# An attention, dense and expert kernel: two exponentials, value loads and mixing matrices issued in another order, and the routing's sums and counting rearranged

## The chip, the cores and the metric

The kernel runs on one core of a Trainium2 chip. The metric is the device time of one execution in microseconds. Kernels are compared by the median of several runs. All times below are of one core; the profile is of one execution, taken by the hardware profiler.

## The reference: what is computed

Three stages follow each other, all in FP32.

```
scores = q @ k.T / 8                      # 4 batches, 12 heads, 448 rows, 64 wide
scores = einsum("bhij,hg->bgij", scores, w_pre)
attn   = softmax(scores)
attn   = einsum("bhij,hg->bgij", attn, w_post)
x      = attn @ v                         # rows become 1792 tokens of 768
h      = x @ w_in                         # 768 -> 2048
x      = where(h > 0, h, exp(h) - 1) @ w_out          # 2048 -> 768
compute = x @ w_skip > 0
e       = argmax(x @ w_gate)              # 8 experts
out     = x;  for tokens with compute:
out    += prob[e] * (relu(x @ w1[e]) @ w2[e])         # 768 -> 1024 -> 768
```

The heads are mixed by two 12 x 12 matrices, once before and once after the softmax. A token with a skip score of zero or less passes unchanged; all others go to the one expert with the largest logit.

## The kernel before, in words

**Precision.** A matrix is held as two parts, a high one and the rest, and a product is three matmuls (high with high, high with low, low with high: `THREE`, L38). Splitting is a cast on ScalarE and a subtraction on VectorE or GpSimd.

**Attention** (L72 to L430) goes through tiles of 120, 120, 120 and 88 query rows of each batch, and each tile in three periods (48 periods). The scores of a tile (`qk`, L144, six matmuls for each of two heads, two PSUM tiles) are written to `s` and brought by DMA into a layout where rows and heads share the partitions (`d`, `relayout`, L183). A period handles up to two pairs of blocks, `cur[0]` and `cur[1]`. For each pair: `mix_pre` (L201) multiplies by the first mixing matrix (`kpre_low`, `kpre_up`) into PSUM tiles `c`; `top` (L211) takes row maxima on VectorE (`nmx`); `softmax` (L218) takes two exponentials on ScalarE (`e`, with the sums `sm`); `norm` (L227) scales the second mixing matrix by the sums (`kr`). In the next period `mix_post` (L240) multiplies `e` by `kr` into `f`, and two copies, one on ScalarE and one on VectorE, put it into `at` (L258). Between the second pair and its `norm` the same loop issues the `qk` of a later tile, and then `av` (L261), the product with the values `v`. The PSUM tiles of `c` and `qk` share one pool of five buffers, `ps_w` (L101): a period takes eight, so the last `qk` tiles use buffers that this period's exponentials have just read.

All loads, relayouts and stores are issued by SyncE (SP) in the order of the program. At the start SyncE issues the loads of q and k, of the mixing matrices and of all v of the first batch (L333); `kron` (L299) and L355 to L366 build the mixing matrices on VectorE and GpSimd after the first tile's scores.

**The dense stage.** h is computed in groups of 128 features by 448 tokens (`products`, L579; 18 matmuls each). The weights come as 64 bit floats, `narrowing` (L480) makes FP32 of them (`a`, `p`, `wf`), `split` (L460) the two parts. `split_x` (L521) splits the tokens `x` into `xh`.  The order of the first eight groups is written out by hand (L666 to L697).

**The second dense product and the routing** (L703 to L908) go through 14 tiles of 128 tokens. A tile has 16 chunks of six matmuls (`o`, L859), and its results are copied to `x2` by ScalarE. Weights that did not stay on the chip come back through DRAM (`wr`, L804). During a tile the one before it is routed: `score` (L740 on) makes nine sums of 768 products each, six on VectorE (L755), three as a product on GpSimd (L748) and a sum on ScalarE (L749); `route` (L759 on) finds the best expert, a one-hot row `oh` (L776), and counts how many tokens went to each expert so far with two matmuls `pp` (L778, L779); the slots are then written to DRAM by an indirect DMA (L797). The tiles 12 and 13 alternate by chunks at the end. For the last two tiles the first expert's tokens are not fetched back: one-hot matrices `hot` and transposes (`tx`, `pt`) place them, and the older ones come by a gather `xp` (L864) from rows that the slots name (`pre`, L877).

From the second dense product on a scheduler sets the order of the instructions on each engine from their dependences and its own estimates; up to group 7 of the dense stage the program's order stands.

**The experts** follow, with weights `w1t` loaded ahead.

Of the kernel before, what the change touches and what calls it, by code (L numbers as in the profile page):

```python
# [20 lines left out]
NK = DM // 128  # L21
# [27 lines left out]
AT_SCORE, AT_ROUTE, AT_FIRST = 8, 18, 11  # L49

# [21 lines left out]
def attention(tc, q, k, v, w_pre, w_post, xT, mix):  # L72
# [12 lines left out]
    with ExitStack() as ctx, ExitStack() as mixing, ExitStack() as scoring:  # L85
# [175 lines left out]
        def av(T, u, ps=None):  # L261
# [15 lines left out]
            for p in (2 * u, 2 * u + 1):  # L277
                if b + 1 < B and it == len(ROWS) - 1:
                    load_v(b + 1, p)
# [7 lines left out]
        stores = []  # L287
# [45 lines left out]
        for p in range(NK):  # L333
            load_v(0, p)
        moves = []
        for p in range(NK):
            if p + 1 < NK:
                if p % 2:
                    split_q(0, p // 2 + 1)
                split_k(0, p + 1, nc.vector)  # L340
            move = qk(0, p)
            if p > 0:
                moves.pop()()
            moves.append(move)
        moves.pop()()
# [6 lines left out]
        kpre = kron(pre, "kpre", False)  # L352
        kpost = kron(post, "kpost", True)

        kpre_low = const.tile([UP, UP], FP32, name="kpre_low")  # L355
        nc.vector.memset(kpre_low, 0.0)
        nc.sync.dma_start(out=kpre_low[GAP:, GAP:], in_=kpre[:HP, :HP])
        kpre_up = const.tile([128, UP], FP32, name="kpre_up")
        nc.sync.dma_start(out=kpre_up[UP:UP + HP, :], in_=kpre[:HP, :UP])
        kposts = [const.tile([128, HP], FP32, name=f"kpost{z}") for z in range(2)]  # L360
        for t in kposts:
            nc.vector.memset(t, 0.0)
        nc.vector.tensor_copy(out=kposts[1][:HP].rearrange("p (g i) -> p g i", g=H),
                              in_=kpost[:HP].rearrange("p (g i) -> p g i", g=H)[:, :, :HR])
        for z, first in ((1, UP), (0, GAP), (0, UP + GAP)):
            nc.sync.dma_start(out=kposts[z][first:first + HP, :], in_=kposts[1][:HP, :])  # L366
# [5 lines left out]
        for n in range(NP):  # L372
# [11 lines left out]
            if late:  # L384
                next(mix)
            if T2 < len(tiles):
                if u2 == 0:
                    load_q(T2)
                if tiles[T2][1] == 0:
                    load_k(tiles[T2][0], 2 * u2)  # L390
                    load_k(tiles[T2][0], 2 * u2 + 1)
            scores = []
            for i in range(2):
                mix_pre(cur[i])
                if i == 0 and n + 2 < NP:
                    relayout(units[n + 2][0])
                moves = mix_post(old[i]) if old else []
                top(cur[i])
                if old:
                    moves[1](nc.scalar.copy)  # L400
                    moves[0](nc.vector.tensor_copy)
                softmax(cur[i])
                if i == 1 and T < len(tiles):
                    scores = [qk(T, 2 * u), qk(T, 2 * u + 1)]
                if late:
                    next(mix)
# [28 lines left out]
def mixtures(tc, order, xT, w_in, w_out, w_skip, w_gate, w1, w2, ident, gT, wf, wg, x2d, slots, out):  # L435
# [5 lines left out]
    with ExitStack() as top:  # L441
# [27 lines left out]
        with ExitStack() as ctx:  # L469
            f64_p = pool("f64", 2, ctx, side="right")  # L470
            cv_p = pool("cv", 1, ctx, side="right")
            xr_p = pool("xr", 6, ctx, side="right")
# [193 lines left out]
            narrowed[1] = narrow(raws.pop(1))  # L666
            raws["out"] = load_w_out(0)
            products(1)
            split_x(2, range(3), both)
            elu(1)  # L670
            wi[1] = split(narrowed.pop(1), ring_a)
            split_x(2, range(3, 6), both)
# [33 lines left out]
        with ExitStack() as ctx:  # L706
# [33 lines left out]
            def score(x2, cols=slice(0, DM)):  # L740
# [3 lines left out]
                for e in range(E + 1):  # L744
                    w = wrow[:, e, cols]
                    if e % 3 == 0:
                        p = st_p.tile([128, DM], FP32, tag="prod", name="prod", bufs=2)
                        nc.gpsimd.tensor_tensor(out=p[:, :n], in0=x2, in1=w, op=ALU.mult)  # L748
                        nc.scalar.activation(out=p[:, :n], in_=p[:, :n], func=ACTF.Copy, accum_out=lg[:, e:e + 1])  # L749
                    else:  # L750
                        if part == 0:
                            t = st_p.tile([128, DM], FP32, tag="junk", name="junk", bufs=1)
                        o = part * n
                        part = (part + 1) % (DM // n)
                        nc.vector.scalar_tensor_tensor(out=t[:, o:o + n], in0=x2, scalar=1.0, in1=w, op0=ALU.mult,  # L755
                                                       op1=ALU.mult, accum_out=lg[:, e:e + 1])
                return lg

            def route(i, lg):  # L759
# [16 lines left out]
                nc.vector.tensor_scalar(out=oh, in0=iota8, scalar1=ef, scalar2=do, op0=ALU.is_equal, op1=ALU.mult)  # L776
                pp = ps_r.tile([128, 512], FP32, tag="r", name="pp")
                nc.tensor.matmul(out=pp[:, :E], lhsT=ones, rhs=seen, start=True, stop=False)  # L778
                nc.tensor.matmul(out=pp[:, :E], lhsT=upper, rhs=oh, start=False, stop=True)  # L779
# [68 lines left out]
            for i, n, fc, cs in work:  # L848
# [24 lines left out]
                if i and n == (15 if i == 1 else AT_ROUTE if last else 11):  # L873
                    hot = old_hot = route(i - 1, scored if last else score(rows[i - 1]))
# [7 lines left out]
                if fc == NF - 1:  # L882
                    if 0 in cs:
                        x2 = rows[i] = x2_p.tile([128, DM], FP32, tag="x2", name="x2")
                    for c in cs:
                        to, at = x2[:, cols[c]], po[c][:, :cols[c].stop - cols[c].start]
                        if last and c == 0:
                            nc.vector.tensor_copy(out=to, in_=at)
                        else:
                            nc.scalar.copy(out=to, in_=at)  # L890
# [9 lines left out]
            hot = route(NTILE - 1, lg)  # L900
# [416 lines left out]
```

## Time and profile before

| | |
|---|---|
| median of 3 runs | 1108.67 us (1106.9 to 1115.65) |
| the profiled execution | 1108.77 us, span 1107.0 us |
| mean granted clock of TensorE | 0.981 |
| TensorE busy | 1024.1 us, 93% |
| VectorE busy | 802.3 us, 72% |
| ScalarE busy | 566.7 us, 51% |
| GpSimd busy | 390.7 us, 35% |
| attention | to about 400 us |
| first dense product | about 400 to 652 us |
| second dense product, routing | about 652 to 924 us |
| experts | about 924 to 1107 us |

A matmul row counts an engine as busy while a matmul runs; matmuls on different halves of the array can run side by side. The idle time in front of an instruction is put down to the instruction of another engine, or the DMA, that came last among those it waited for. Times in rows are microseconds from the start of the span.

### The profile page before, as it was taken

What the parts mean: (1) busy time and instruction counts of PE and PEld (TensorE: products, weight loads), DVE (VectorE), ACT (ScalarE), POOL (GpSimd) and SP (SyncE); (2) the same over time, 40 slices, a digit from 0 to 9 for tenths busy, and PEclk for the clock granted to TensorE, in tenths of its full rate; (3) what the DMA queues carried; (4) which work ended last, traced back from release to release, by engine and by line L of the source; (5) the groups of instructions that cost most, each with busy time, mean ns of one, the idle gap of its engine ahead of it and who ended that gap; (6) DMA issues with size and microseconds to landing.
All of it is one profiled execution on the core that took longest, in us unless ns stands there. A gap on an engine that the chain in (4) does not pass through costs nothing. (4 is left out here: it accounts for less than half of the span.)

```text
span 1107.0 us, 29935 instructions
## 1 busy us (share of the span) xinstructions
PE 1024.1 (93%) x12082; PEld 882.8 (80%) x12082; DVE 802.3 (72%) x1495; ACT 566.7 (51%) x1150; POOL 390.7 (35%) x355
## 2 busy tenths in 40 slices
PE   6998999899899888999999999999999989899997
PEld 4676667666677667899999988999999978788887
DVE  5775777677577668667666557878787856999953
ACT  5664656466465555444544454333333326677751
POOL 2232214123221226232232202535354534756521
PEclk8999999999999999999999999999999998999999
DMA  6453564465455556555566557733333385999800
GB/s 202 170 173 109 164 202 138 131 195 182 110 165 173 166 153 225 171 170 157 193 215 206 178 171 262 237 94 107 96 105 107 94 317 184 392 391 343 328 8 32
DMA packets 134218, 199.67 MB, mean 180 GB/s; under 512 B 35860, under 2 KB 101400, under 8 KB 133821
## 3 DMA queue, kind: packets, MB, share of 16 engines
q1 hardware_dynamic: 131933, 191.27, 52.4%
q0 software_dynamic: 2144, 6.46, 1.6%
q8 instruction: 96, 1.57, 0.6%
q14 instruction: 45, 0.37, 0.1%
HBM read 122.47 MB, written 37.65 MB: 145 GB/s over the span
## 5 line engine op out<-in xcount | busy, mean ns | idle before, releaser
L859 PE MATMUL o<-w,gh 128*128 128x384 f32 (+2 forms) x1344 | 242.5, 339 | 2.9 <-ACT w L463 2.4
L585 PE MATMUL h<-xh,w 128*128 128x448 f32 x1152 | 236.3, 367 | 4.7 <-POOL xh L519 4.7
L859 PEld LDWEIGHTS o<-w,gh 128*128 128x128 f32 x1344 | 234.1, 190 | 7.3 <-ACT w L463 3.6
L585 PEld LDWEIGHTS h<-xh,w 128*128 128x128 f32 x1152 | 216.9, 189 | 23.4 <-POOL xh L519 6.5
L236 POOL TENSOR_SCALAR kr<-kpost,rs 128x60 f32<-128x60 f32 x180 | 77.4, 444 | 284.5 <-DVE rs L232 242.7
L252 PEld LDWEIGHTS f<-kr,e 64*64 64x64 f32 (+2 forms) x5760 | 121.2, 138 | 54.6 <-issue 33.5
L755 DVE SCALAR_TENSOR_TENSOR junk<-x,wrow 128x768 f32<-128x768 f32 x78 | 117.1, 1501 | 40.0 <-ACT x L890 38.6
L252 PE MATMUL f<-kr,e 64*64 64x60 f32 (+2 forms) x5760 | 122.4, 225 | 7.3 <-DVE at L258 1.8
L500 POOL TENSOR_TENSOR wf<-a,p 128x768 f32<-128x768 f32 x32 | 66.6, 2082 | 163.3 <-DVE p L498 122.8
L215 DVE TENSOR_REDUCE nmx<-c 128x1 f32<-128x448 f32 x180 | 104.5, 620 | 25.9 <-PE c L206 25.9
L258 ACT COPY at<-f 128x480 f32<-128x480 f32 x96 | 52.5, 547 | 135.2 <-PE f L252 135.2
L1029 DVE TENSOR_TENSOR wlo<-w1t,whi 128x1536 fp32r<-128x1536 f32 x50 | 111.6, 2255 | 13.6 <-ACT whi L1026 13.6
L224 ACT ACTIVATE e<-c,nmx 128x448 f32<-128x448 f32 x180 | 113.0, 637 | 6.3 <-DVE nmx L215 6.3
L1026 ACT CAST whi<-w1t 128x1536 fp32r<-128x1536 f32 x64 | 94.3, 1483 | 34.1 <-PE ph L1056 17.5
L748 POOL TENSOR_TENSOR prod<-x,wrow 128x768 f32<-128x768 f32 x39 | 93.9, 2434 | 50.0 <-ACT x L890 26.8
L154 PE MATMUL qk<-k,qq 64*120 64x448 f32 (+1 forms) x576 | 90.6, 404 | 17.3 <-ACT e L224 10.3
L206 PE MATMUL c<-d,kpre_up 60*64 60x448 f32 x336 | 85.1, 574 | 11.7 <-ACT s L158 11.7
L274 PE MATMUL xp<-at,v 128*64 128x120 f32 (+3 forms) x1536 | 92.2, 267 | 1.4 <-DVE at L258 1.4
L274 PEld LDWEIGHTS xp<-at,v 128*64 128x64 f32 (+1 forms) x1536 | 75.1, 137 | 21.9 <-issue 17.3
L159 DVE TENSOR_SCALAR s<-qk 120x448 f32<-120x448 f32 (+1 forms) x96 | 58.3, 618 | 45.0 <-PE qk L154 19.8
L206 PE MATMUL c<-d,kpre_low 64*64 64x448 f32 x336 | 84.3, 554 | 3.5 <-DMA kpre_low<-kpre_kr 3.5
L154 PEld LDWEIGHTS qk<-k,qq 64*120 64x120 f32 (+1 forms) x576 | 52.8, 180 | 42.1 <-ACT e L224 25.2
(185 smaller groups left out, 1449.2 us busy)
## 6 DMA issues: line engine op xcount, KB each, us to landing
w1t<-in_moe_w_dram SPq DMA_DIRECT2D x64, 768.0 KB
d<-s SPq DMA_DIRECT2D x168, 210.0 KB
gT<-g SPq DMA_DIRECT2D x64, 224.0 KB
f<-in_moe_w_in_dram SPq DMA_DIRECT2D x16, 768.0 KB
f<-in_moe_w_out_dram SPq DMA_DIRECT2D x16, 768.0 KB
gr<-gT SPq DMA_DIRECT2D x48, 256.0 KB
rk<-in_k_dram SPq DMA_DIRECT2D x24, 224.0 KB
xr<-xT SPq DMA_DIRECT2D x24, 224.0 KB
```

The lines of the kernel that those rows point to most:

```text
L154: nc.tensor.matmul(out=ps[:n, :S], lhsT=qt[T, p // 2][rows, a, p % 2, :n], rhs=kt[b, p][rows, z, :], start=(i == 0), stop=(i == 2))
L206: nc.tensor.matmul(out=ps[j * UP:(j + 1) * UP, :S], lhsT=kpre_up[UP:UP + HP, :] if z else kpre_low if len(U) == 2 else kpre[:d[z, j].shape ...
L215: nc.vector.tensor_reduce(out=t, in_=c, op=ALU.max, axis=AX.X, negate=True)
L224: nc.scalar.activation(out=e, in_=c, func=ACTF.Exp, bias=t, accum_out=sms[U][:, i:i + 1])
L252: nc.tensor.matmul(out=ps[to, c // 2, :, z, :], lhsT=e[rows, keys], rhs=kr[rows, :])
L274: nc.tensor.matmul(out=ps[z * 64:(z + 1) * 64, i, :n], lhsT=t[:, z, jc % t.shape[2], :], rhs=att[T][:t.shape[0], jc, 2 * p + z, :n], start ...
L585: nc.tensor.matmul(out=ps, lhsT=w[:, a, kk, :], rhs=xs[tb, kk][:, z, :], start=(kk == 0 and a + z == 0), stop=(kk == NK - 1 and a == 1))
L748: nc.gpsimd.tensor_tensor(out=p[:, :n], in0=x2, in1=w, op=ALU.mult)
L755: nc.vector.scalar_tensor_tensor(out=t[:, o:o + n], in0=x2, scalar=1.0, in1=w, op0=ALU.mult, op1=ALU.mult, accum_out=lg[:, e:e + 1])
L859: mm = nc.tensor.matmul(out=po[c][:, :cols[c].stop - cols[c].start], lhsT=gs[i][fc // GC][:, a, fc % GC, :], rhs=wo[fc][:, z, cols[c]], st ...
L1026: nc.scalar.copy(out=hi, in_=t)
L1029: (nc.vector if dve else nc.gpsimd).tensor_tensor(out=lo, in0=t, in1=hi, op=ALU.subtract)
```

## The change

In attention, three things move. The loads of v are put on a list (`values`) and issued in the next period, behind that period's relayouts and stores and ahead of the loads of q and k; for the first batch this is behind the relayouts of the first two periods. The mixing matrices are built within the loop of the first tile's scores. And for the second pair of a period the two exponentials are issued ahead of the copy `at<-f` on ScalarE.

In the dense stage the pool `xr` has nine buffers instead of six, and all of `split_x(2)` stands ahead of the second weight block's `narrow`. In the routing all nine sums are made on VectorE; `route` is cut in two, and its second part `seat`, with the counting matmuls, comes at chunk 15 instead of 11 (for the last tile both stay at 18); the last tile's first copy of `x` goes from VectorE to ScalarE.

```diff
@@ attention
+                values.append((b + 1, p))          # was: load_v(b + 1, p)
...
-        for p in range(NK):
-            load_v(0, p)
+        values += [(0, p) for p in range(NK)]
         for p in range(NK):
...
             moves.append(move)
+            if p == 2:
+                kpre = kron(pre, "kpre", False)
+                kpost = kron(post, "kpost", True)
...
         split_q(1, 1)
-        kpre = kron(pre, "kpre", False)
-        kpost = kron(post, "kpost", True)
...
         relayout(units[1][0])
@@ the loop over periods
                 next(mix)
+            while values:
+                load_v(*values.pop(0))
             if T2 < len(tiles):
...
                 moves = mix_post(old[i]) if old else []
                 top(cur[i])
+                if i == 1:
+                    softmax(cur[i])
                 if old:
                     moves[1](nc.scalar.copy)
                     moves[0](nc.vector.tensor_copy)
-                softmax(cur[i])
+                if i == 0:
+                    softmax(cur[i])
@@ the dense stage
-            xr_p = pool("xr", 6, ctx, side="right")
+            xr_p = pool("xr", 9, ctx, side="right")
...
-            narrowed[1] = narrow(raws.pop(1))
             raws["out"] = load_w_out(0)
             products(1)
-            split_x(2, range(3), both)
+            split_x(2, range(6), both)
+            narrowed[1] = narrow(raws.pop(1))
             elu(1)
             wi[1] = split(narrowed.pop(1), ring_a)
-            split_x(2, range(3, 6), both)
             load_x(3)
@@ score: all nine sums
-                    if e % 3 == 0:
-                        p = st_p.tile([128, DM], FP32, tag="prod", name="prod", bufs=2)
-                        nc.gpsimd.tensor_tensor(out=p[:, :n], in0=x2, in1=w, op=ALU.mult)
-                        nc.scalar.activation(out=p[:, :n], in_=p[:, :n], func=ACTF.Copy, accum_out=lg[:, e:e + 1])
-                    else:
...
+                    nc.vector.scalar_tensor_tensor(out=t[:, o:o + n], in0=x2, scalar=1.0, in1=w, op0=ALU.mult,
+                                                   op1=ALU.mult, accum_out=lg[:, e:e + 1])
@@ route is cut in two
+                return i, oh, do
+
+            def seat(i, oh, do, after=None):
                 pp = ps_r.tile([128, 512], FP32, tag="r", name="pp")
...
-                if i and n == (15 if i == 1 else AT_ROUTE if last else 11):
-                    hot = old_hot = route(i - 1, scored if last else score(rows[i - 1]))
+                if i and n == (AT_ROUTE if last else 11):
+                    routing = route(i - 1, scored if last else score(rows[i - 1]))
+                if i and n == (AT_ROUTE if last else AT_SEAT):
+                    hot = old_hot = seat(*routing, None if last else mm)
...
-                        if last and c == 0:
-                            nc.vector.tensor_copy(out=to, in_=at)
-                        else:
-                            nc.scalar.copy(out=to, in_=at)
+                        nc.scalar.copy(out=to, in_=at)
```

The order of ScalarE in one period of attention, before (`at<-f` is the copy of the finished product, `e` an exponential, `s` a copy of scores, `qq` a split of q):

```order
L258 COPY at<-f 128x48x10
L224 ACTIVATE e,sm<-c,nmx 128x448 x2
L258 COPY at<-f 128x48x4
L224 ACTIVATE e,sm<-c,nmx 128x448 x2
L158 ACTIVATE s<-qk 120x448 x2
L141 CAST qq<-rq 128x240
```

and now:

```order
L259 COPY at<-f 128x48x10
L225 ACTIVATE e,sm<-c,nmx 128x448 x4
L259 COPY at<-f 128x48x10
L159 ACTIVATE s<-qk 120x448 x2
L142 CAST qq<-rq 128x240
```

All four exponentials now stand together, and the second copy `at<-f` behind them.

The order of SyncE at the start, before, from the last load of v on (`d` are relayouts of scores, four for a first pair; `kpre` and `kpost` parts of the mixing matrices):

```order
L125 DMA v<-in_v_dram 64x128
L193 DMA d_154<-s 120x1x448
L193 DMA d_155<-s 120x1x448
L193 DMA d_156<-s 120x1x448
L193 DMA d_157<-s 120x1x448
L112 DMA rq<-in_q_dram 128x720
L357 DMA kpre_low<-kpre_kr 60x60
L359 DMA kpre_up<-kpre_kr 60x64
L366 DMA kpost_330<-kpost_330 60x60
L366 DMA kpost_329<-kpost_330 60x60 x2
L193 DMA d_158<-s 120x1x448
```

and now, from the last part of the mixing matrices on:

```order
L360 DMA kpost_252<-kpost_253 60x60 x2
L194 DMA d_154<-s 120x1x448
L194 DMA d_155<-s 120x1x448
L194 DMA d_156<-s 120x1x448
L194 DMA d_157<-s 120x1x448
L113 DMA rq<-in_q_dram 128x720
L194 DMA d_158<-s 120x1x448
L194 DMA d_159<-s 120x1x448
L194 DMA d_160<-s 120x1x448
L194 DMA d_161<-s 120x1x448
L126 DMA v<-in_v_dram 128x384
```

The five DMAs of the matrices now stand ahead of the first `d`, and the twelve loads of v behind the eighth.

The order of VectorE in a token tile of the routing, before, from the slots on (`gh` is a split of the next tile's input, `junk` a sum):

```order
L796 CAST si<-slot 128x1
L736 TENSOR_TENSOR gh<-gr,gh 128x512
L755 SCALAR_TENSOR_TENSOR junk,lg<-x_11734,wrow 128x768
L736 TENSOR_TENSOR gh<-gr,gh 128x512
L755 SCALAR_TENSOR_TENSOR junk,lg<-x_11734,wrow 128x768 x3
L736 TENSOR_TENSOR gh<-gr,gh 128x512
L755 SCALAR_TENSOR_TENSOR junk,lg<-x_11734,wrow 128x768 x2
L761 MAX mx<-lg 128x8
```

and now:

```order
L802 CAST si<-slot 128x1
L755 SCALAR_TENSOR_TENSOR junk,lg<-x_11713,wrow 128x768
L741 TENSOR_TENSOR gh<-gr,gh 128x512
L755 SCALAR_TENSOR_TENSOR junk,lg<-x_11713,wrow 128x768 x3
L741 TENSOR_TENSOR gh<-gr,gh 128x512
L755 SCALAR_TENSOR_TENSOR junk,lg<-x_11713,wrow 128x768 x4
L741 TENSOR_TENSOR gh<-gr,gh 128x512
L755 SCALAR_TENSOR_TENSOR junk,lg<-x_11713,wrow 128x768
L761 MAX mx<-lg 128x8
```

Nine sums stand where six stood; the fourth `gh` of a tile is ahead of this piece in both.

## Rows read from the trace of the kernel before

**Rows 1.** The page, part 1: busy us (share of the span) and instructions of TensorE.

```profile
PE 1024.1 (93%) x12082; PEld 882.8 (80%) x12082; DVE 802.3 (72%) x1495; ACT 566.7 (51%) x1150; POOL 390.7 (35%) x355
```

**Rows 2.** The waits of TensorE: released by what, us in total, times, longest.

```profile
engine line waited for: us in total, times, longest us
...
PE qk L154 <- ACT e L224: 10.3, 31, 0.4
PE pp L779 <- DVE oh L776: 8.3, 10, 1.5
...
PE h L585 <- POOL xh L519: 4.7, 3, 4.1
PE tx L844 <- DVE load L930: 4.6, 1, 4.6
PE c L206 <- DMA kpre_low<-kpre_kr: 3.5, 1, 3.5
...
PE o L859 <- ACT w L463: 2.4, 3, 1.9
```

**Rows 3.** Time line of TensorE, a period with the wait: start, us, instructions, [idle before].

```profile
126.44 1.07 PE L154 MATMUL qk<-k,qq 64*120 64x448 f32 x7
127.84 0.88 PE L154 MATMUL qk<-k,qq 64*120 64x448 f32 x5 [0.32 <-ACT e L224]
128.64 0.59 PE L274 MATMUL xp<-at,v 128*64 128x88 f32 x9
```

**Rows 4.** The same, a period without the wait.

```profile
92.93 1.48 PE L154 MATMUL qk<-k,qq 64*120 64x448 f32 x12
94.34 0.84 PE L274 MATMUL xp<-at,v 128*64 128x120 f32 x12
```

**Rows 5.** Time line of ScalarE and VectorE in the period of rows 3.

```profile
125.27 1.16 DVE L215 TENSOR_REDUCE nmx<-c 128x1 f32<-128x448 f32 x2
...
125.58 0.64 ACT L224 ACTIVATE e<-c,nmx 128x448 f32<-128x448 f32 x1
...
126.60 0.57 ACT L258 COPY at<-f 128x480 f32<-128x480 f32 x1 [0.29 <-PE f L252]
...
127.06 0.63 ACT L224 ACTIVATE e<-c,nmx 128x448 f32<-128x448 f32 x1
...
127.68 0.64 ACT L224 ACTIVATE e<-c,nmx 128x448 f32<-128x448 f32 x1
```

**Rows 6.** Time line of SyncE at the start: DMA issues.

```profile
7.45 6.93 SPq L125 DMA_DIRECT2D v<-in_v_dram  x12
...
18.77 0.85 SPq L357 DMA_DIRECT2D kpre_low<-kpre_kr  x1
```

**Rows 7.** Time line of ScalarE, first token tile of the second dense product.

```profile
661.25 1.68 ACT L463 CAST w<-wr 128x768 fp32r<-128x768 f32 x2 [1.62 <-DMA wr<-wf]
```

**Rows 8.** Stretches: busy us and instructions of each engine, granted clock, DMA share, GB/s.

```profile
core 0: us, PE busy (x) PEld busy (x) DVE busy (x) ACT busy (x) POOL busy (x), PEclk, DMA share, GB/s
...
705.70:709.10 3.40, 3.40 (x12) 3.40 (x11) 2.56 (x6) 1.32 (x2) 0.00 (x0) 0.50 0.87 253
...
742.40:760.50 18.10, 17.35 (x100) 17.26 (x100) 14.57 (x31) 6.12 (x15) 8.59 (x4) 1.00 0.34 101
```

**Rows 9.** Groups by line, VectorE, one token tile (742.5 to 760.6): busy us, mean ns.

```profile
L755 DVE SCALAR_TENSOR_TENSOR junk<-x,wrow 128x768 f32<-128x768 f32 x6 | 8.9, 1483 | 3.2 <-ACT x L890 3.1
```

**Rows 10.** Line 755 over the whole kernel: ns of one, minimum/median/maximum.

```profile
L755 DVE SCALAR_TENSOR_TENSOR junk<-x,wrow x78: 946/959/2620, 678.4 to 909.6; 128x768 f32<-128x768 f32 x78
```

**Rows 11.** Time lines of GpSimd and VectorE in one token tile.

```profile
711.70 7.37 POOL L748 TENSOR_TENSOR prod<-x,wrow 128x768 f32<-128x768 f32 x3 [1.09 <-ACT x L890]
...
717.42 2.47 DVE L755 SCALAR_TENSOR_TENSOR junk<-x,wrow 128x768 f32<-128x768 f32 x1
```

**Rows 12.** Time lines of GpSimd, VectorE and TensorE at the end of the routing.

```profile
899.39 1.05 POOL L864 DMA_INDIRECT xp<-x2d,pre  x1 [6.69 <-DMA pre<-slots]
...
910.49 0.68 DVE L888 COPY x<-o 128x512 f32<-128x512 f32 x1
...
916.26 0.41 PE L830 MATMUL pt<-ident,xp 128*128 128x128 f32 x1
```

**Rows 13.** DMA issues from 888 to 925: median us from issue to landing.

```profile
xp<-x2d,pre POOLq DMA_INDIRECT x1, 7.4
```

More of the change, by code (lines that the diff above doesn't have):

```diff
@@ L49 @@
 AT_SCORE, AT_ROUTE, AT_FIRST = 8, 18, 11
+AT_SEAT = 15
 R0, RC, LOOK = 3, 2, 2
@@ L285, in av @@
             return move
-        stores = []
+        stores, values = [], []
         def store():
@@ L344, in attention @@
             moves.append(move)
+            if p == 2:
+                kpre = kron(pre, "kpre", False)
+                kpost = kron(post, "kpost", True)
+                kpre_low = const.tile([UP, UP], FP32, name="kpre_low")
+                nc.vector.memset(kpre_low, 0.0)
+                nc.sync.dma_start(out=kpre_low[GAP:, GAP:], in_=kpre[:HP, :HP])
+                kpre_up = const.tile([128, UP], FP32, name="kpre_up")
+                nc.sync.dma_start(out=kpre_up[UP:UP + HP, :], in_=kpre[:HP, :UP])
+                kposts = [const.tile([128, HP], FP32, name=f"kpost{z}") for z in range(2)]
+                for t in kposts:
+                    nc.vector.memset(t, 0.0)
+                nc.vector.tensor_copy(out=kposts[1][:HP].rearrange("p (g i) -> p g i", g=H),
+                                      in_=kpost[:HP].rearrange("p (g i) -> p g i", g=H)[:, :, :HR])
+                for z, first in ((1, UP), (0, GAP), (0, UP + GAP)):
+                    nc.sync.dma_start(out=kposts[z][first:first + HP, :], in_=kposts[1][:HP, :])
         moves.pop()()
@@ L351, in attention @@
         split_q(1, 1)
-        kpre = kron(pre, "kpre", False)
-        kpost = kron(post, "kpost", True)
[L355 to L366, printed above, removed]
         relayout(units[1][0])
@@ L745, in score @@
                     w = wrow[:, e, cols]
-                    if e % 3 == 0:
-                        p = st_p.tile([128, DM], FP32, tag="prod", name="prod", bufs=2)
-                        nc.gpsimd.tensor_tensor(out=p[:, :n], in0=x2, in1=w, op=ALU.mult)
-                        nc.scalar.activation(out=p[:, :n], in_=p[:, :n], func=ACTF.Copy, accum_out=lg[:, e:e + 1])
-                    else:
[L751 to L756, printed above, removed]
+                    if part == 0:
+                        t = st_p.tile([128, DM], FP32, tag="junk", name="junk", bufs=1)
+                    o = part * n
+                    part = (part + 1) % (DM // n)
+                    nc.vector.scalar_tensor_tensor(out=t[:, o:o + n], in0=x2, scalar=1.0, in1=w, op0=ALU.mult,
+                                                   op1=ALU.mult, accum_out=lg[:, e:e + 1])
                 return lg
@@ L776, in route @@
                 nc.vector.tensor_scalar(out=oh, in0=iota8, scalar1=ef, scalar2=do, op0=ALU.is_equal, op1=ALU.mult)
+                return i, oh, do
+            def seat(i, oh, do, after=None):
                 pp = ps_r.tile([128, 512], FP32, tag="r", name="pp")
-                nc.tensor.matmul(out=pp[:, :E], lhsT=ones, rhs=seen, start=True, stop=False)
-                nc.tensor.matmul(out=pp[:, :E], lhsT=upper, rhs=oh, start=False, stop=True)
+                with behind(after):
+                    nc.tensor.matmul(out=pp[:, :E], lhsT=ones, rhs=seen, start=True, stop=False)
+                with behind(after):
+                    nc.tensor.matmul(out=pp[:, :E], lhsT=upper, rhs=oh, start=False, stop=True)
                 nc.vector.tensor_tensor(out=seen, in0=seen, in1=oh, op=ALU.add)
@@ L899, in mixtures @@
                             nc.sync.dma_start(out=out[i * 128:(i + 1) * 128, :], in_=x2)
-            hot = route(NTILE - 1, lg)
+            hot = seat(*route(NTILE - 1, lg))
             place_old(range(5, NK))
```

1 line of the change is left out of this document (removed).

## The prediction

> **What bounds the kernel now.** I read the page first, then the waits of TensorE, then the time lines around the longest of them. The page says that TensorE is busy for 1024.1 us of 1107.0 [rows 1], so at most 83 us can come from its idle time, unless matmuls that count as busy become shorter. The waits [rows 2] put names to the idle time that this change can reach: qk for an exponential (10.3 us, 31 times), the counting matmul pp for the one-hot row oh (8.3, 10 times), h for xh (4.7), tx in the tail (4.6), c for kpre_low (3.5), o for the split weights w (2.4). All other engines matter only where one of these waits ends on them.
>
> **The exponential in attention.** This term is the largest, and the 10.3 us of the waits is not its size. In a period that does not stall, the twelve qk matmuls start at 92.93 and the next work at 94.34, 1.41 us later [rows 4]; they run in pairs side by side. In a period that stalls, seven start, the eighth waits 0.32, and the next work starts at 128.64, 2.20 us after 126.44 [rows 3]: the wait also breaks the pairs apart. So one stall costs 2.20 - 1.41 = 0.79 us, and 31 of them 24.5 us.
>
> What ends it: the eighth matmul needs the PSUM buffer that the first exponential of the second pair reads (127.06, 0.63 long, ending 127.69; the matmul starts 0.15 later) [rows 3, 5]. Ahead of that exponential ScalarE waits for f and makes a copy at<-f (126.60, 0.57) [rows 5]. The change puts both exponentials ahead of this copy. The first can then start when the exponential before it lets it, 0.62 us after 125.58 (the pitch of 127.06 to 127.68), at 126.20; the maxima are no hindrance, since the first of the two that take 1.16 us from 125.27 is done about 125.9 [rows 5]. It ends at 126.83, and the buffer is free at 126.98. Without a stall the eighth matmul pairs with the seventh, which is due 0.71 us into the group, at 127.15 (the pitch of 1.41 us in six pairs, the first of them longer; an estimate from rows 4). The margin is 0.17 us, small, but the periods repeat alike.
>
> What is late next is the copy: after two exponentials it runs from 127.43 to 128.00. Values' matmuls would now start at 126.44 + 1.41 = 127.85. In every third period they read the tile that this copy completes, and wait some 0.24 us with the release; 10 such periods give back 2.4 us. The two copies of qk behind it start by 127.9 instead of 128.37, so they are not later. The term is -24.5 + 2.4 = **-22.1**. Its bounds are -24.5 (no new wait) and about -8 (the release comes late and only the 0.3 us of idle of each stall is won, less the 2.4).
>
> **The start.** Before, SyncE issues twelve loads of v in 6.93 us ahead of the d relayouts, and kpre_low at 18.77, for which TensorE waits 3.5 us [rows 2, 6]. The change puts the mixing matrices first (five DMAs, some 0.8 us each by the distance in rows 6) and v behind the d of the first two periods. The wait for kpre_low goes, but VectorE and the d relayouts get the matrices' operations ahead of them, and the 6.93 us of v now stand ahead of the d of the third period. Bounds: -3.5, the whole wait, and +3.5, a new wait of that size there. I take **-0.5**.
>
> **The dense stage's first sums.** TensorE waits 4.7 us for xh [rows 2], which GpSimd makes behind wf. The change makes all six xh first. Then wf, and with it the split of the second weight block, comes later, and the fourth product needs that one. So most of the wait moves to the weights: **-1**, between -4.7 and +1.
>
> **The reloaded weights.** ScalarE's cast w waits 1.62 us for the DMA wr<-wf [rows 7], which SyncE issues behind the last gT stores. With the first tile's work in another order these loads go out between those stores, ahead of the last one. I count the whole 2.4: **-2.4**, at worst 0.
>
> **The sums and the counting.** A token tile takes 18.10 us, of which TensorE works 17.35 and VectorE 14.57 [rows 8]; the 0.75 that TensorE lacks are the wait for oh. The change gives VectorE nine sums instead of six, takes three products from GpSimd, and puts pp four chunks (24 matmuls of 17.35/96 = 0.18 us, 4.3 us) later. What a sum costs: 0.959 us in the median and 2.62 at most [rows 10]; six make 8.9 us in a tile [rows 9], and the long ones lie beside the GpSimd products: 2.47 us at 717.42, while three products run for 7.37 us from 711.70 [rows 11]. These products go, so I price all nine at 0.96: 14.57 - 8.9 + 9 x 0.96 + 3 x 0.08 = 14.6 us, without counting that gh gets faster too. Sums start about 0.9 us into the tile, so oh is ready by 15.5, ahead of pp near 17.3. The wait goes: **-8.3** (10 waits). The first long one of these is followed by 3.40 us at half clock (0.50, 1.2 GHz) [rows 8], which would take half that at full: **-1.7**, at worst 0.
>
> **The tail.** TensorE waits 4.6 us for tx; the engine named is VectorE's `load`, but what tx reads is the copy x<-o, which VectorE reaches at 910.49 behind six sums [rows 2, 12]. On ScalarE it comes some 3.9 us sooner (4.6 less a copy of 0.68). But the counting of tile 11 also falls 8 chunks back here, since two tiles alternate: 48 x 0.18 = 8.7 us. The gather xp, issued at 899.39 and 7.4 us on its way, then lands at 899.39 + 8.7 + 7.4 = 915.5, and pt<-xp, before at 916.26, could run at 912.4 [rows 12, 13]. So about 3 of the 3.9 us become a wait for the gather: **-1**, between -5 and +5 (a later gather, and a slow clock after the wait).
>
> **Sum:** -22.1 - 0.5 - 1 - 2.4 - 8.3 - 1.7 - 1 = -37.0. The profiled execution took 1108.77 us (span 1107.0), 0.1 above the median of 1108.67, so no correction: 1108.8 - 37.0 = **1071.8**, I say 1072. The experts behind it are gated by the routing and should only start earlier.
>
> **The rivals.**
> *The stall in attention moves and stays (chance 0.13).* ScalarE's copy at<-f, or its copies of qk behind it, hold values' matmuls or the next c by as much as the exponential held qk. For it: ScalarE does the same work in the same period, and the margin was 0.17 us. Against: two periods in three do not read that copy at once, and the copies of qk come no later than before. The -22.1 becomes about 0 to -3: 1092.
>
> *VectorE becomes the bound in routing (0.04; the other side).* Its place is each of the 12 tiles from 690 to 905. The budget is 14.57 - 8.9 + 9t + 0.24 with t the price of a sum; it passes TensorE's 17.35 at t = 1.27 us. At today's mean of 1.48 [rows 9] it is 19.2, which is 1.9 x 12 = 23 us dearer than the forecast, 1095: no change by much. From t = 1.6 the change is slower. Were half of the nine as long as 2.47 us [rows 11], t is 1.71, a tile takes 21.3, and the time is 1072 + 3.95 x 12 = 1119. Against it: half of today's sums take no more than 0.959 us [rows 10], and the products, beside which the long one stands [rows 11], are what goes. The Trainium skill (Perfetto Trace Analysis, Identifying the Most-Contended Engine) takes an engine's occupancy as a fair measure of how near VectorE is to its limit and would have the fullest engine relieved first. By that rule a VectorE at 14.57 of 18.10 should get no third more sums, and it would choose this rival. Another page (SBUF — State Buffer, Who interferes with whom) has a VectorE instruction with two SBUF inputs contend with a GpSimd instruction that reads SBUF, which speaks for the short price; here no row shows nine sums without products.
>
> *The edges give back (0.11).* The v loads hold the third period (+3.5 instead of -0.5) and the gather comes late with a slow clock (+5 instead of -1): 1072 + 4 + 6 = 1082.
>
> **How the numbers follow.** The forecast has 0.72. Its own bounds reach from 1062 (no wait at the copy, the tail and the start at their good ends) to about 1083. The range goes up to 1092 to take in the third rival and the middle of the first; what is left out is the rest of the first, the second, and sums beyond the bounds below. A measurement of this kernel tells about 1% from no change, 11 us: all but the second rival, and the worst of the first, are faster by more. Faster 0.93, same 0.04, slower 0.03.
>
> **What would show it.** Right: qk no longer among the waits, twelve qk in 1.41 us, attention shorter by about 22 us; sums of 0.96 without exception; no wait for oh before the last tiles and a tile of 17.35 us; tx without its 4.6 us, and pt<-xp waiting for the gather instead. Wrong: values' matmuls or c waiting for ScalarE's copies 0.5 us or more in each period; sums above 1.3 us; a wait for d near 32 us above 3; o waiting for gh because VectorE is full.

## The result and the profile after

The changed kernel takes 1084.36 us in the median of 4 runs (1082.25 to 1085.37); before takes 1111.3 in 4 runs. The ratio is 0.9745, 95% interval 0.9705 to 0.9785: faster, and inside the range of 1062 to 1092, but 12 us above the forecast of 1072 and just outside the forecast's own bounds (1062 to about 1083): the range holds it because it was widened for the rivals. The profiled execution has a span of 1082.3 us, 24.7 less than before, where 37.0 were forecast.

The page, part 1, and the waits of TensorE in the changed kernel (columns as in [rows 1, 2]):

```profile
PE 1017.3 (94%) x12082; PEld 884.1 (82%) x12082; DVE 778.0 (72%) x1573; ACT 531.6 (49%) x1073; POOL 301.1 (28%) x315
```

```profile
engine line waited for: us in total, times, longest us
PE c L207 <- ACT s L159: 14.0, 4, 4.0
PE pt L836 <- DMA xp<-x2d,pre: 6.2, 1, 6.2
...
PE h L591 <- ACT w L469: 3.3, 1, 3.3
...
PE c L207 <- DMA d<-s: 2.3, 1, 2.3
PE xp L275 <- ACT at L259: 1.8, 4, 1.0
...
PE f L253 <- issue: 1.7, 4, 0.6
...
PE o L865 <- ACT w L469: 0.9, 1, 0.9
...
PE qk L155 <- ACT e L225: 0.5, 2, 0.4
```

The waits for `oh` (8.3 us) of [rows 2] are gone, and so are those for `kpre_low` and `tx`; of those for `e` (10.3) 0.5 us is left, in the first period. New at the top stand the gather `xp` (6.2), a fourth wait of `c` for ScalarE's copy of scores, and `d`; h waits for weights instead of xh.

The period of [rows 3, 5], now; first TensorE, then ScalarE:

```profile
128.64 1.49 PE L155 MATMUL qk<-k,qq 64*120 64x448 f32 x12
130.06 0.45 PE L275 MATMUL xp<-at,v 128*64 128x88 f32 x6
```

```profile
128.38 0.65 ACT L225 ACTIVATE e<-c,nmx 128x448 f32<-128x448 f32 x1
...
129.00 0.65 ACT L225 ACTIVATE e<-c,nmx 128x448 f32<-128x448 f32 x1
...
129.60 0.59 ACT L259 COPY at<-f 128x480 f32<-128x480 f32 x1
130.05 1.02 ACT L159 ACTIVATE s<-qk 120x448 f32<-120x448 f32 x2
```

Twelve qk in one piece, 1.42 us to the next work instead of 2.20. The first exponential of the second pair starts 0.26 us ahead of the qk group, where it stood 0.62 us behind its start.

A token tile of the routing, and the sums over the whole kernel (columns as in [rows 8, 10]):

```profile
709.20:726.38 17.18, 17.18 (x103) 17.18 (x102) 12.74 (x38) 3.64 (x9) 1.43 (x1) 1.00 0.36 108
```

```profile
L755 DVE SCALAR_TENSOR_TENSOR junk<-x,wrow x117: 947/957/1008, 660.0 to 880.8; 128x768 f32<-128x768 f32 x117
```

A tile takes 17.18 us instead of 18.10, without idle time on TensorE. No sum is longer than 1.01 us, and VectorE is busy for less (12.74 us) with nine sums than it was with six (14.57).

To see where the 12 us went I took the same matmul in both traces (their counts agree for every kind) and noted by how much the changed kernel is ahead of it:

| from / to (time before) | ahead at its end | this piece | forecast for it |
|---|---|---|---|
| start to qk of the fourth period (45.4) | +3.7 | +3.7 | -2.1 (-0.5, and two stalls of 0.79) |
| to the first h (399.8) | -10.5 | -14.2 | -20.5 (the rest of -22.1) |
| to the fifth group of h (429.3) | -10.3 | +0.2 | -1 |
| to the last h (650.0) | -11.4 | -1.1 | 0 |
| first tile, reloaded weights (674.8) | -13.9 | -2.6 | -2.4 |
| tiles 1 to 11 (873.6) | -27.0 | -13.0 | -10.0 (-8.3 and -1.7) |
| tail, to the first expert matmul (924.4) | -24.8 | +2.1 | -1 |
| experts | -24.8 | 0.0 | 0 |

Three pieces lost against the forecast, the start 5.8, attention 6.3 and the tail 3.1 us; the tiles won 3.0 more.

### The profile page after: what moved, and what is told of

It is laid out like the page before. It is cut to its first block, busy times and chain, and to the rows that moved or that the text cites. A ratio compares the mean times of both kernels' runs of the same rounds, so it can differ in the third digit from the quotient of the medians.

```text
span 1082.3 us, 29868 instructions
## 1 busy us (share of the span) xinstructions
PE 1017.3 (94%) x12082; PEld 884.1 (82%) x12082; DVE 778.0 (72%) x1573; ACT 531.6 (49%) x1073; POOL 301.1 (28%) x315
## 5 line engine op out<-in xcount | busy, mean ns | idle before, releaser
L865 PE MATMUL o<-w,gh 128*128 128x384 f32 (+2 forms) x1344 | 238.9, 337 | 1.3 <-ACT w L469 0.9
L253 PEld LDWEIGHTS f<-kr,e 64*64 64x64 f32 (+2 forms) x5760 | 124.3, 139 | 56.3 <-issue 38.5
L237 POOL TENSOR_SCALAR kr<-kpost,rs 128x60 f32<-128x60 f32 x180 | 80.1, 459 | 274.9 <-DVE rs L233 212.1
L253 PE MATMUL f<-kr,e 64*64 64x60 f32 (+2 forms) x5760 | 126.1, 226 | 6.7 <-issue 1.7
L755 DVE SCALAR_TENSOR_TENSOR junk<-x,wrow 128x768 f32<-128x768 f32 x117 | 111.8, 956 | 5.6 <-DMA wrow<-wg 3.1
L155 PE MATMUL qk<-k,qq 64*120 64x448 f32 (+1 forms) x576 | 80.6, 407 | 8.8 <-ACT k L134 5.1
L207 PE MATMUL c<-d,kpre_low 64*64 64x448 f32 x336 | 86.5, 554 | 2.3 <-DMA d<-s 2.3
L740 ACT CAST gh<-gr 128x512 fp32r<-128x512 f32 x56 | 34.9, 624 | 99.6 <-PE o L865 39.4
L160 DVE TENSOR_SCALAR s<-qk 120x448 f32<-120x448 f32 (+1 forms) x96 | 57.4, 617 | 35.0 <-DMA xT<-x 13.6
L803 POOL DMA_INDIRECT slots<-pairs,si x14 | 19.0, 1354 | 227.9 <-DVE si L802 194.4
```

The source lines that it names most:

```text
L155: nc.tensor.matmul(out=ps[:n, :S], lhsT=qt[T, p // 2][rows, a, p % 2, :n], rhs=kt[b, p][rows, z, :], start=(i == 0), stop=(i == 2))
L207: nc.tensor.matmul(out=ps[j * UP:(j + 1) * UP, :S], lhsT=kpre_up[UP:UP + HP, :] if z else kpre_low if len(U) == 2 else kpre[:d[z, j].shape ...
L237: nc.gpsimd.tensor_scalar(out=kr, in0=kposts[i] if k == 2 else kposts[1], scalar1=rs[:, i:i + 1], scalar2=None, op0=ALU.mult)
L253: nc.tensor.matmul(out=ps[to, c // 2, :, z, :], lhsT=e[rows, keys], rhs=kr[rows, :])
L865: mm = nc.tensor.matmul(out=po[c][:, :cols[c].stop - cols[c].start], lhsT=gs[i][fc // GC][:, a, fc % GC, :], rhs=wo[fc][:, z, cols[c]], st ...
```

## The experiments

Each row: median, ratio to before on the same chip with its interval, and four pieces of the table above from the kernel's own profile (of the others, the piece to the last h is +3.1 to +3.6 in e3, e4 and e7 and -1.2 to -0.2 in the rest, e3 has +2.2 at the experts, and e10 has +1.5 at the first groups of h). The order of the exponentials in attention is the same in all but before, and the piece varies between -13.0 and -17.2; differences smaller than that are not read from it.

| kernel | us | ratio | start | attention | tiles | tail |
|---|---|---|---|---|---|---|
| changed | 1084.36 | 0.9745 (0.9705 to 0.9785) | +3.7 | -14.2 | -13.0 | +2.1 |
| e1 exponential alone | 1095.35 | 0.9853 (0.9795 to 0.9911) | +0.2 | -15.2 | 0.0 | -1.0 |
| e2 start as before | 1079.07 | 0.9679 (0.9631 to 0.9726) | -1.1 | -13.3 | -13.0 | +1.6 |
| e3 tile 11 counted early | 1077.5 | 0.9655 (0.9614 to 0.9695) | +3.2 | -14.6 | -13.0 | -7.6 |
| e4 v loads spread | 1079.06 | 0.9678 (0.9627 to 0.9729) | -3.8 | -13.0 | -13.0 | +1.8 |
| e5 sums without late counting | 1073.94 | 0.9685 (0.9647 to 0.9722) | +2.8 | -17.2 | -12.8 | -7.7 |
| e6 late counting without sums | 1081.62 | 0.9747 (0.9694 to 0.98) | +3.2 | -16.2 | -12.5 | +0.2 |
| e7 dense order as before | 1085.49 | 0.9761 (0.9727 to 0.9795) | +3.7 | -16.7 | -12.9 | +1.0 |
| e8 three mends | 1070.65 | 0.9626 (0.9596 to 0.9657) | -4.1 | -14.4 | -13.0 | -7.6 |
| e9 changed, again | 1083.6 | 0.9741 (0.969 to 0.9791) | +3.4 | -14.5 | -13.0 | +2.0 |
| e10 without start and late counting | 1072.49 | 0.9653 (0.9601 to 0.9705) | -0.6 | -16.4 | -11.1 | -6.1 |
| e11 e5 with the copy on VectorE | 1079.55 | 0.9707 (0.964 to 0.9773) | +3.4 | -13.6 | -11.7 | -5.5 |

**e1, the exponential alone.** Before, and in the loop over periods only:

```diff
                 top(cur[i])
+                if i == 1:
+                    softmax(cur[i])
                 if old:
...
-                softmax(cur[i])
+                if i == 0:
+                    softmax(cur[i])
```

> The kernel before with the two exponentials of the second pair ahead of the copy at<-f, and nothing else. Theory A (the term of 22 us is right, the loss is elsewhere): twelve qk in 1.41 us in some 28 periods, a wait of 0.2 us before values' matmuls in every third, and 18 to 22 us less than before, about 1089 to 1093 where before is 1111. Theory B (the attention term itself was too large, because periods bound each other elsewhere): at most 12 us less, 1099 or more.

Measured: 1095.35, 19.2 us less than before on the same chip, and a span 16.0 us shorter in the profile. By the times alone this is not settled: the interval of the ratio, 0.9795 to 0.9911, is a gain of 10 to 23 us and takes in both theories. The profile speaks for A in the mechanism and for a little less in the size. From the fourth period on the qk groups together (first qk to the next work) are 21.4 us shorter than before, as forecast, but the stage only 15.2. Six microseconds come back within attention itself (below).

**e2, the start as before.**

```diff
-        values += [(0, p) for p in range(NK)]
+        for p in range(NK):
+            load_v(0, p)
...
-            if p == 2:
-                kpre = kron(pre, "kpre", False)
...
         split_q(1, 1)
+        kpre = kron(pre, "kpre", False)
```

> The changed kernel with the start as before: the loads of v ahead of the first d relayouts, the mixing matrices after the first tile's scores; later loads of v stay moved. Theory A (the moved start costs 4.5 us: waits of 2.3 us each for d and for ScalarE's copy of scores near 34 and 37 us, and a half-clock stretch there): the third period starts about 5 us sooner, 4 to 5 us less than the changed kernel's 1084.4, about 1080; TensorE's wait of 3.5 us for kpre_low is back. Theory B (the start is even, the waits are compensated by the earlier first c): within 1.5 us of 1084.4.

**e4, the v loads spread.**

```diff
-            while values:
-                load_v(*values.pop(0))
+            for _ in range(2 if n else 0):
+                if values:
+                    load_v(*values.pop(0))
```

> The changed kernel with the first batch's loads of v spread: two heads (four DMAs, about 2.5 us of SyncE) in each period from the second on, instead of all twelve in the first. Theory A (the twelve loads, 7.8 us on SyncE, hold the d of the third period): no wait for d near 34 us, no half-clock stretch there, 4 to 5 us less than 1084.4. Theory B (the matrices' place is what costs at the start: VectorE waits 1.28 us for GpSimd in the middle of the scores): less than 1.5 us.

Both are theory A. The start piece falls by 4.8 us in e2 and by 7.4 in e4 (more than the 4 to 5 expected there), the ratio by 0.7% in both; the intervals still overlap that of the changed kernel, so the sizes are those of the profiles. TensorE in the third period, of the changed kernel, then of e4:

```profile
33.98 0.93 PE L207 MATMUL c<-d,kpre_low 64*64 64x448 f32 x2 [2.33 <-DMA d<-s]
37.25 1.01 PE L207 MATMUL c<-d,kpre_up 60*64 60x448 f32 x1 [2.34 <-ACT s L159]
```

```profile
30.14 1.48 PE L155 MATMUL qk<-k,qq 64*120 64x448 f32 x12
31.55 0.59 PE L207 MATMUL c<-d,kpre_low 64*64 64x448 f32 x1
```

SyncE in the changed kernel, then in e4:

```profile
23.23 7.76 SPq L126 DMA_DIRECT2D v<-in_v_dram  x12
31.10 7.08 SPq L194 DMA_DIRECT2D d<-s  x8
```

```profile
19.79 6.76 SPq L194 DMA_DIRECT2D d<-s  x8
26.61 3.43 SPq L126 DMA_DIRECT2D v<-in_v_dram  x4
30.22 3.52 SPq L194 DMA_DIRECT2D d<-s  x4
```

A period has four d, two for each of its two pairs. With the twelve loads ahead, the d of the third period are issued from 31.10 on, as the first four of these eight; in e4 they are the last four of the eight from 19.79 on, and those at 30.22 belong to the fourth period. The first wait draws the second: ScalarE's copies of scores write the tile that late d relayouts still read (both engines wait 5.5 us for `d<-s` until 36.65), and the next c needs their buffers. A stretch at half clock from 34.95 to 41.78 lies over both; e4 has none there. Before has a stretch of the same length too, behind its wait for kpre_low. Stretches of before, of the changed kernel and of e4 (columns as in [rows 8]):

```profile
19.62:26.45 6.83, 4.67 (x22) 2.94 (x23) 2.22 (x4) 1.74 (x5) 0.00 (x0) 0.50 0.41 135
```

```profile
34.95:41.78 6.83, 4.53 (x80) 3.07 (x84) 3.52 (x8) 2.24 (x5) 0.83 (x2) 0.50 0.72 245
```

```profile
29.94:36.77 6.83, 6.58 (x179) 4.81 (x175) 5.96 (x15) 5.61 (x18) 1.67 (x4) 1.00 0.67 211
```

So the change took one wait with a slow stretch away and set two waits with another in its place. What cost was v as one block of twelve. With the loads spread, the new start is worth having: e4 is 2.7 us ahead of e2 at the fourth period. These two differ in the place of the matrices and in that of v, so how much each gives there is not shown.

**e3, tile 11 counted early.**

```diff
-                if i and n == (AT_ROUTE if last else AT_SEAT):
+                if i and n == (AT_ROUTE if last else 11 if i == OLD else AT_SEAT):
```

> The changed kernel with the counting of tile 11 at chunk 11 instead of 15 (tiles 12 and 13 alternate there, so it stands some 8.7 us earlier), all others at 15. Theory A (the gather xp is late because the counting is late): TensorE's wait of 6.2 us for xp goes, the stretch at half clock behind it (13.65 us) shrinks or goes, and 8 to 11 us less: about 1075. Theory B (something else holds the tail, such as the copies on ScalarE or the landing of the slots): less than 3 us.

Measured: the tail is 9.7 us shorter than the changed kernel's, theory A. The ratio is 0.9% lower, some 10 us, and the two intervals do not overlap. The span of the profile is only 4.5 us shorter, since two things take some back in it: the gather of an expert's tokens is late (4.4 us, row below), and h runs at a slower pitch, as the last section tells.

```profile
913.78 0.84 PE L1049 MATMUL pt<-ident,xg 128*128 128x128 f32 x6 [4.43 <-DMA xg<-x2d,ids]
```

The chain in the changed kernel (time lines of TensorE and GpSimd), and the gather's consumer in e5, where the counting is early too:

```profile
873.21 1.43 POOL L803 DMA_INDIRECT slots<-pairs,si  x1 [24.12 <-DVE si L802]
880.99 1.74 POOL L870 DMA_INDIRECT xp<-x2d,pre  x1 [6.35 <-DMA pre<-slots]
...
888.75 1.22 PE L836 MATMUL pt<-ident,xp 128*128 128x128 f32 x4 [6.17 <-DMA xp<-x2d,pre]
```

```profile
878.11 0.60 PE L836 MATMUL pt<-ident,xp 128*128 128x128 f32 x4
```

From the slots' DMA to the first use of the gather pass 15.5 us, and all of the tail behind the wait then runs at half clock, 884.87 to 898.52 (same columns as [rows 8]):

```profile
884.87:898.52 13.65, 9.05 (x39) 8.55 (x40) 2.63 (x23) 2.38 (x6) 1.36 (x2) 0.50 0.37 134
```

**e5 and e6, the two halves of the routing's change.** e5 sets `AT_SEAT = 11`; e6 keeps 15 and puts the three products back on GpSimd:

```diff
+                    if e % 3 == 0:
+                        p = st_p.tile([128, DM], FP32, tag="prod", name="prod", bufs=2)
+                        nc.gpsimd.tensor_tensor(out=p[:, :n], in0=x2, in1=w, op=ALU.mult)
+                        nc.scalar.activation(out=p[:, :n], in_=p[:, :n], func=ACTF.Copy, accum_out=lg[:, e:e + 1])
+                    else:
...
```

> The changed kernel with the counting back at chunk 11 for every tile: of the routing's two changes only the sums on VectorE are left (and the last tile's copy). Theory A (the sums end ahead of chunk 11 once no product lies beside them: start 0.9, nine of 1.0 us, four gh and small work, 13.3 us into the tile against some 12.4 at chunk 11): a wait for oh of 0 to 1 us per tile stays, and since the gather comes early as in e3 the tail gains 6 to 8 us; 1076 to 1084. Theory B (the late place is what removed the waits, and the sums are now later than before by three): waits of 1 to 3 us in each of 10 tiles, 1085 to 1105.

> The changed kernel with three of the nine products on GpSimd again: of the routing's two changes only the late counting is left. Theory A (the late place alone hides oh; today's oh comes 0.76 us late and 4.3 us are given): no wait for oh in the tiles, 17.2 us per tile, but the last tiles' sums of 2.5 us each are back; 1084 to 1090. Theory B (the sums have to be on VectorE too): waits of about 0.8 us in 10 tiles are back, 1092 or more.

Either half alone removes every wait for `oh` in the tiles (none is left between 690 and 850 us in either), and both give tiles of 17.2 us: -12.8 and -12.5 where the two together give -13.0. One tile of e5, then of e6:

```profile
700.33:717.51 17.18, 17.18 (x102) 17.18 (x101) 12.66 (x38) 3.64 (x8) 1.18 (x1) 1.00 0.36 107
```

```profile
717.20:734.40 17.20, 17.20 (x102) 17.20 (x101) 15.55 (x32) 6.13 (x14) 6.91 (x4) 1.00 0.36 108
```

In e5 oh is done at 717.18 and the counting that reads it starts at 717.65, so it fits by 0.5 us. The late place is then not needed, and it is what costs the tail: e5's tail is 9.8 us shorter than the changed kernel's. Both medians lie below what theory A gave, 1073.94 under 1076 to 1084 and 1081.62 under 1084 to 1090: e5 kept no wait for `oh` at all, and attention is 2 to 3 us shorter in these two profiles, within its spread. By the times alone e6 is unclear (0.9694 to 0.98, single runs from 1074.78 to 1090.09), so the reading is that of its profile. In e6 the tail has none of e5's gain, since ScalarE's copy of x stands behind its own sums of the products, and tx waits for it:

```profile
880.56 1.11 PE L855 MATMUL tx<-ident,x 128*128 128x128 f32 x4 [3.70 <-ACT x L900]
```

**e11, the last copy.** e5 with the line `nc.vector.tensor_copy(out=to, in_=at)` back for the last tile's first copy.

> The kernel of e5 (counting at chunk 11) with the last tile's first copy of x back on VectorE, behind the nine sums. Theory A (the copy's engine is what frees tx): the copy comes when the sums end, some 3 us later than ScalarE's, TensorE waits some 3 us for tx and goes to half clock, 3 to 6 us more than e5. Theory B (the slow sums beside GpSimd's products were the cause, the engine does not matter): within 1 us of e5's tail, which is 7.7 us shorter than before.

Between the two theories: the copy comes at 880.09, behind six sums, and the tail is 2.2 us longer than in e5 (-5.5 against -7.7). The wait of 3 us for tx that theory A expected is not there. Of the tail's gain the copy's engine has the smaller part. The medians lie further apart (1079.55 and 1073.94), but start and attention, which the two kernels share, make 4.2 us of that in the profiles.

**e7, the dense order as before** (`narrow` first, `split_x(2)` in two halves, six buffers).

> The changed kernel with the dense stage's first groups in the order of before (weights' narrowing ahead of the tokens' split, six buffers). Theory A (the wait for xh only became a wait for the weights, 4.1 against 3.3 + 0.3 us): within 2 us of 1084.4, TensorE waits about 4 us for xh again. Theory B (the change won what was read off as the wait for xh): 3 to 4 us more than 1084.4.

Theory A: the first groups of h end at +0.2 in both kernels. TensorE waits 4.6 us for xh again; the changed kernel waits for w instead (3.3 and 0.3 us) and 0.3 for xh, 3.9 together, and the 0.7 us between them does not show at the end of these groups. The median, 1085.49, would say the same, but two other pieces stand against each other in it (attention -16.7, h +3.6). But one thing nobody asked for: the gain at the reloaded weights, -2.6 in the changed kernel, is +0.2 here. In e7's order `wr<-wf` stands behind the last gT store again; in the changed kernel three of its seven loads go out ahead of that store. SyncE in the changed kernel, then in e7:

```profile
635.44 0.33 SPq L811 DMA_DIRECT2D wr<-wf  x1
...
642.61 0.33 SPq L602 DMA_DIRECT2D gT<-g  x1
```

```profile
644.50 0.38 SPq L602 DMA_DIRECT2D gT<-g  x1
...
647.98 1.28 SPq L812 DMA_DIRECT2D wr<-wf  x3
```

The waits of e7 from 640 to 680 us:

```profile
PE o L866 <- ACT w L469: 2.6, 2, 1.5
PE o L866 <- DVE w L470: 0.2, 1, 0.2
```

So that gain belongs to the dense stage's edit, by way of the scheduler, which sets the order from there on.

**e9, e10, e8: together.** e9 is the changed kernel again; e10 joins e2 and e5; e8 joins e3 and e4 and builds the second mixing matrix where it was.

> The changed kernel as it is, once more, to stand beside the next two on the same chip: 1082 to 1087, with the waits of its first profile (6 us for the gather xp, 2.3 us each near 34 and 37 us). A theory that these waits were of one execution only would show other ones here.

> The changed kernel without the two parts that the experiments found to cost: the start as before (e2) and the counting at chunk 11 for every tile (e5). What is left is the exponential's place, the dense stage's order, the nine sums and the last copy. If the losses of e2 and e5 are separate (4.9 and 9.8 us in the profiles), it is 13 to 16 us faster than e9. If one hides the other, or the experts take it back, 8 to 11.

> The changed kernel with three mends together: the first batch's v loads spread over periods (e4), the second mixing matrix built where it was before so that VectorE does not wait 1.28 us for GpSimd among the scores, and the counting of tile 11 at chunk 11 (e3). If the three losses are independent the profile starts the third period 8 us sooner than the changed kernel and the tail is 6 us shorter: 1068 to 1073. If the later stages take the gain back (a gather of the experts that is late by 4.4 us in e3): 1074 to 1078.

e9 repeats the changed kernel in time and in waits (6.3 us for xp, 2.3 for d). e10 is 11.1 us faster than e9 on the same chip (0.9653 against 0.9741), short of the 13 to 16: start and tail give 4.0 and 8.1, less than the 4.8 of e2 and the 9.8 of e5, and the tiles 1.9 less. What the tiles lack lies in one place: the counting of the first tile, which before and the changed kernel put at chunk 15, stands at chunk 11 here, and TensorE waits 1.5 us for it (`pp`, put down to `issue`); in e11, with the same place, it waits 0.9, in e5 not at all. e8 has the lowest ratio, 0.9626 (0.9596 to 0.9657; 1070.65 us, 1063.72 to 1071.31 in 6 runs), wholly below the changed kernel's interval and overlapping those of e3 and e10. Its start is only 0.3 us ahead of e4's, so in these two profiles the place of the second matrix, and the 1.28 us that VectorE waits for it, matters little.

## Why the prediction was right, and where it was off

**The exponential.** Right in mechanism and, for the qk groups, in size: from the fourth period on they are 20.2 us shorter, against 20.5 forecast with the wait in every third period. That wait is there, 0.2 us where 0.24 was forecast (1.60 to the next work instead of 1.40), but in 6 periods and not in 10:

```profile
142.09 1.49 PE L155 MATMUL qk<-k,qq 64*120 64x448 f32 x12
143.69 0.53 PE L275 MATMUL xp<-at,v 128*64 128x120 f32 x6
```

The margin of 0.17 us held, except in one period after each batch boundary (three times, 0.4 us left: 1.82 to the next work), and one group ran at half clock (2.52 us, at 113 us). These take what the fewer waits save, so that the sum agrees to 0.3 us is partly luck. The step that failed is taking these 20 us as the stage's gain. 6.0 of them come back (6.2 in e1, which has this change alone). In part they are waits that no other engine ends: `issue` in this stage goes from 0.2 to 2.8 us. The rest may go with the clock: TensorE spends 30.0 us of this stage at half clock (0.50, 1.2 GHz) instead of 17.1; at the first batch boundary, whose wait of 4.0 us is as long as before, the stretch is 10.24 us long (3.41 before); before, then now:

```profile
108.37:111.78 3.41, 3.41 (x76) 2.26 (x71) 2.62 (x8) 1.07 (x4) 0.43 (x1) 0.50 0.67 190
```

```profile
106.63:116.87 10.24, 9.43 (x130) 7.02 (x132) 6.71 (x18) 5.47 (x14) 1.27 (x3) 0.50 0.60 205
```

The 9.43 us of work in it would take some 4.7 us at full clock, where before 3.41 us were slow. That the two make up the 6.0 is worked out, not shown by an experiment. The share of each is not fixed: in e3 and e10 the time at half clock is nearly that of before (20.0 and 19.5 us), `issue` is 6.4 and 5.7, and 6.7 and 5.1 us come back. What makes TensorE wait there stays open.

**The start.** The forecast was -0.5 with +3.5 as the far end; it is +5.3 (3.7, and the 1.6 of two stalls that also went). I had the mechanism, v ahead of the third period's d, and priced it as one wait. It was two of 2.3 us, the second drawn by the first through the copies of scores, and a stretch at half clock over both. The forecast had no slow stretch on either side, and the one that before has behind its wait for kpre_low went. With both new waits gone (e4) the piece is -3.8, or -2.2 without the stalls, which lies between the bounds.

**The dense stage and the reloaded weights.** +0.2 instead of -1, and -2.6 as forecast (-2.4), but this is luck: the reason was not the routing's new order but the dense stage's edit (e7).

**The sums and the counting.** The price of 0.96 us held for all 117 sums. The tiles gave -13.0 instead of -10.0: each became 0.92 us shorter, where the forecast had 0.83 (8.3 over 10), and the first wait of 1.2 us (put down to `issue`) went too, which I had left out. What failed is the claim behind it that the late place is part of the gain. Without it the tiles are as fast (e5).

**The tail.** Right in mechanism: pt waits for the gather, 6.2 us where some 3 were forecast. The chain from pp to the landing was as long as reckoned; TensorE came to pt earlier than I thought, since all of the work ahead of it now ran at full clock (before, the 4.9 us from tx to pt lay in a stretch at half clock, 910.5 to 920.74). The 4.6 us before tx went, but because the sums became short; the engine of the copy has 2.2 us of it (e11).

**The rivals.** The first (the stall stays) did not come. The second did not come either: VectorE took three more sums and became less busy, 12.74 us instead of 14.57 of a tile, since part of its time was waiting for GpSimd in the guise of work. The prediction had the Trainium skill (Perfetto Trace Analysis, Identifying the Most-Contended Engine) on the side of this rival, by its rule to relieve the fullest engine first. That was misread: in the same section the Trainium skill judges TensorE by its rate of arithmetic and the busy share of its weight loads. Its weight loads are busy for 17.26 of 18.10 us [rows 8], above VectorE's 14.57, so the rule names TensorE here. The Trainium skill (SBUF — State Buffer, Who interferes with whom) has a VectorE instruction with two SBUF inputs contend with a GpSimd instruction that reads SBUF. The rows agree: a sum takes 0.957 us in the median without the products and never above 1.01, and up to 2.62 with them. The third (start and tail both late) is nearest to what came, though I gave it 0.11: its time was 1082, and 1084 was measured. That the two times are so near is in part luck: it has neither the 6.0 us that attention gave back nor the 3.0 that the tiles won.

## What to carry to other kernels

A wait of 0.3 us in a group of matmuls that run in pairs can cost 0.8, so read the price of a stall from a period without it, not from the idle time; and do not book the sum of these prices as the gain of the stage, of which 6 of 20 us came back here. When a fix has two halves, run each alone: here either half removed the wait, and the second only brought its own cost at the end, where two tiles alternate and four chunks are eight. And loads that "have time" must be counted on the queue of what is needed next: twelve issues in one place delayed a transfer that four of them in each period did not (e4).

## What the runs showed of the hardware

- In e6 one sum took 6.65 us, the whole series of products beside it, where before two or three sums of 2.5 us alternated with them. The series takes 5.44 us on GpSimd then, less than before (7.37, [rows 11]).

```profile
709.22 5.44 POOL L753 TENSOR_TENSOR prod<-x,wrow 128x768 f32<-128x768 f32 x3
```

```profile
708.83 6.65 DVE L760 SCALAR_TENSOR_TENSOR junk<-x,wrow 128x768 f32<-128x768 f32 x1
```

- The h matmuls, the same code in all kernels, have a median pitch of 0.202 us in most profiles and 0.207 in those of e3, e4 and e7; behind the eighth group the granted clock is 1.00 in all. The stage takes some 4 us longer with it (253.3 to 254.1 instead of 249.0 to 251.1 from the first h to the last). The repeats of e3 (1074.83, 1075.46, 1079.55, 1079.65) lie as far apart. What sets it stays open.
- TensorE's waits put down to `issue` in attention went from 0.2 us before to between 2.2 and 7.0 in the kernels with the new order. None of the runs shows why.
